# Keys and queries of later chunks transposed by VectorE instead of TensorE, and step sizes moved onto the keys

## The chip, the core and the metric

One core of a Trainium2 chip runs the whole program. The time is device microseconds of one execution, from the first to the last instruction and the little that lies around it. Three executions of the kernel before are given by their median. Engines are named as the profile names them: PE is TensorE's matmul, PEld its weight load, DVE is VectorE, ACT is ScalarE, POOL is GpSimd, SP is SyncE, which issues nearly all the transfers.

## What is computed

A delta-rule attention (4 batches, 8 heads, 768 positions, head size 48) gives 3072 rows of 384 numbers, which then go through two dense layers of width 2048, the first with mish, the second with hardswish:

```python
k_n = k / (norm(k) + 1e-06)
for t in range(S):
    y[:, :, t] = einsum('bhd,bhde->bhe', q[:, :, t], state)
    v_old = einsum('bhde,bhd->bhe', state, k_n[:, :, t])
    state = state + beta_t * einsum('bhd,bhe->bhde', k_n[:, :, t], v_t - v_old)
x = y reshaped to (3072, 384)
x = mish(x @ moe_w_in) @ moe_w_out            # 384 -> 2048 -> 384
x = hardswish(x @ moe2_w_in) @ moe2_w_out     # 384 -> 2048 -> 384
```

## The kernel before

The 768 positions are cut into 24 chunks of 32. A chunk holds its 4 batches as four groups of 32 partitions. For each chunk `t` the following is done.

- The keys are loaded by `load_heads` (L268, four transfers of 48 KB, one for each batch) into one of five tiles `kpad`, with positions on partitions; the queries go into one of two tiles `qpad`.
- TensorE turns both to have the head's 48 numbers on partitions: `T_pe` (L434) is four 128x128 transposes for the keys and four for the queries, and ScalarE copies each result from PSUM to `kqt` (`T_ew`, L440).
- `G_pe` (L454) multiplies keys with keys and keys with queries, into two PSUM banks. The first product, times the step sizes and a triangular mask `mb`, is the chunk's matrix `an`: VectorE forms it in `G_ew` (L472). The second becomes `mt`: ScalarE copies it (L483) and GpSimd masks it (L622).
- A unit triangular system with `an` is solved by 31 steps. For two chunks at a time, `an` goes to DRAM and back in another layout (`ad`, `ash`), VectorE multiplies (L785) and adds (L792) in each step, and the inverse goes to DRAM and back (`td`, `pt`). GpSimd multiplies `pt` with the step sizes (`scale`, L813).
- The recurrence `rec` then needs TensorE four times: K (`ksps`, L827), U (`ups`, L837), the output MU (`yps`, L847) and the state update S (`dsps`, L879), which VectorE adds to the state `sbd` in eight instructions (L890).

Chunks 0 to 7 are prepared ahead by other routines (`prep_k`, `matrices`, `whole`, `quads`). From chunk 8 on, the transposes of chunk `t + 4` stand directly behind U of chunk `t`, in the variable `tk` of `rec`. There are 16 such chunks.

Four chunks make a block of 512 columns for the dense layers. The first dense layer (phase 1) has six blocks of 16 units, each with nine matmuls into `hps` (L1205) and nine into `o` (L1226). The second (phase 2) begins when phase 1 ends. Before a unit of block 0 can run, its weights must be split into two rounded parts: ScalarE and VectorE do that in `lane` and `part` (L1139 to L1170). VectorE writes the last part of each of 28 pieces as `wil` or `wol` (L1170). The input of a block is split into `xh` (ScalarE) and `xl` (VectorE, L1187), into the same tiles for every block, after the last `hps` matmul of the block before.

All of this is written by one planner, `Flow`. Each routine is a generator that asks for an engine and a duration; the planner takes the request that could begin first, shifted by a penalty (`pen`), and writes its instructions there. So the order on every engine is fixed when the kernel is built, and each engine works through its own list in that order. `landed` and `DVE`/`ACT` numbers are the planner's assumptions of durations; changing them changes the order and nothing else. `warm` writes filler matmuls (L1544) until the first `hps`.

## Time and profile before

| | |
|---|---|
| median of 3 executions | 1038.71 us (1038.07 to 1043.14) |
| the profiled execution | 1040.45 us |
| its span, first to last instruction | 1038.7 us |
| PE busy | 1009.0 us, 97% |
| PEld busy | 842.5 us, 81% |
| DVE busy | 655.6 us, 63% |
| ACT busy | 452.0 us, 44% |
| POOL busy | 119.9 us, 12% |

The profiled execution's own time is 1.7 us over its span, and 1.7 us over the median. The span falls into stages: up to 89 us the first chunks and the first weights, without a dense layer on TensorE; from 89 to about 192 us block 0 of the first dense layer, while its weights are split; to 540 us blocks 1 to 4 with the rest of the attention; to 638 us the end of phase 1; to 1033.5 us phase 2. A share of busy time over the whole span mixes these, so the view of busy times by stretch, the list of waits, and the instructions in order of time around one step are what to read.

### The profile page before, as it was taken

The page shows a single profiled execution, that of the slowest core. Times are in us where ns is not written, and L with a number is a line of the kernel's source. Part 1 is how long each engine was busy: PE and PEld are TensorE (multiplying, and loading weights), DVE is VectorE, ACT ScalarE, POOL GpSimd, SP SyncE. Part 2 cuts the span into 40 slices and gives each one's busy share as a digit, 9 for nine tenths or more (in the row PEclk, how much of TensorE's full clock was granted, in tenths as well). Part 3 has the DMA queues.
Part 4 walks back from the last instruction along what each step waited for, and adds up shares of the span by engine and source line. Part 5 has one row for each costly group of instructions (what it writes and reads, how often), then busy time and mean ns, then how long its engine had stood idle before and what let it go on. Part 6 is the DMA issues. An engine that isn't in the chain of part 4 may idle for free.

```text
span 1038.7 us, 29553 instructions
## 1 busy us (share of the span) xinstructions
PE 1009.0 (97%) x12708; PEld 842.5 (81%) x12730; DVE 655.6 (63%) x1569; ACT 452.0 (44%) x916; POOL 119.9 (12%) x156
## 2 busy tenths in 40 slices
PE   8888999999999999999999999999999999999997
PEld 5466777787777878878778888998999989999997
DVE  7988999976869598596628888333343333433432
ACT  4454666534454354444236665333343333433432
POOL 3242333303121221210000000000000000000000
PEclk9999999999999999999999999999999999999999
DMA  4644553234242434414113643002020020100101
GB/s 87 158 97 103 152 129 99 78 57 77 42 95 41 76 54 87 74 20 89 22 44 121 203 137 107 1 1 62 1 61 1 1 61 1 37 25 1 31 1 32
DMA packets 149124, 66.58 MB, mean 64 GB/s; under 512 B 133088, under 2 KB 136160, under 8 KB 148992
## 3 DMA queue, kind: packets, MB, share of 16 engines
q1 hardware_dynamic: 147664, 64.19, 25.8%
q8 instruction: 100, 1.64, 0.7%
q10 hardware_dynamic: 1328, 0.49, 0.2%
q14 instruction: 32, 0.26, 0.1%
HBM read 51.02 MB, written 13.63 MB: 62 GB/s over the span
## 4 chain that ended last, share of the span: by engine, by line
PE 72%; DVE 16%; issue 2%; ACT 2%; DMA 1%; POOL 0%; SPq 0%; DVEq 0%; ACTq 0%
PE hps L1205 32%; PE p L1364 19%; PE o L1226 12%; DVE tmp L785 3%; DVE sbd L890 3%; DVE tp L792 3%; DVE cv L1147 1%; DVE cv L1150 1%; PE tps L434 1%; PE ksps L827 1%; PE ups L837 1%; PE yps L847 1%; PE dsps L879 1%; PE yps L827 1%; DVE glo L1245 1%
## 5 line engine op out<-in xcount | busy, mean ns | idle before, releaser
L1205 PE MATMUL hps<-xh,wih 128*128 128x512 f32 x576 | 229.5, 398 | 4.7 <-DVE an L472 1.8
L1205 PE MATMUL hps<-xl,wih 128*128 128x512 f32 x576 | 227.5, 395 | 2.3 <-DVE xl L1187 2.2
L1205 PE MATMUL hps<-xh,wil 128*128 128x512 f32 x576 | 227.3, 395 | 0.0
L1339 DVE SCALAR_TENSOR_TENSOR r<-r,hps 128x512 f32<-128x512 f32 x96 | 66.1, 688 | 181.6 <-ACT r L1337 181.4
L1337 ACT ACTIVATE r<-hps,half_c 128x512 f32<-128x512 f32 x96 | 66.1, 689 | 174.8 <-PE hps L1205 174.8
L1205 PEld LDWEIGHTS hps<-xh,wih 128*128 128x128 f32 x576 | 108.7, 189 | 27.5 <-DVE an L472 3.1
L1364 PE MATMUL p<-woh,glo 128*128 128x384 f32 x384 | 129.5, 337 | 0.0
L1364 PE MATMUL p<-woh,ghi 128*128 128x384 f32 x384 | 129.2, 337 | 0.0
L1364 PE MATMUL p<-wol,ghi 128*128 128x384 f32 x384 | 128.9, 336 | 0.0
L1205 PEld LDWEIGHTS hps<-xl,wih 128*128 128x128 f32 x576 | 108.7, 189 | 24.3 <-DVE xl L1187 5.0
L1205 PEld LDWEIGHTS hps<-xh,wil 128*128 128x128 f32 x576 | 108.6, 188 | 23.1
L1236 ACT ACTIVATE g<-hps 128x512 f32<-128x512 f32 x96 | 57.3, 597 | 132.0 <-PE hps L1205 130.2
L1226 PE MATMUL o<-ghi,wol 128*128 128x512 f32 x288 | 114.2, 396 | 0.1
L1226 PE MATMUL o<-ghi,woh 128*128 128x512 f32 x288 | 113.6, 394 | 0.0
L1345 DVE TENSOR_TENSOR glo<-r,ghi 128x512 fp32r<-128x512 f32 x96 | 66.5, 693 | 60.8 <-ACT ghi L1211 60.2
L1245 DVE TENSOR_TENSOR glo<-g,ghi 128x512 fp32r<-128x512 f32 x80 | 56.3, 704 | 75.4 <-ACT ghi L1211 75.0
L1211 ACT ACTIVATE ghi<-r 128x512 fp32r<-128x512 f32 x96 | 60.6, 632 | 70.4 <-DVE r L1339 70.4
L785 DVE TENSOR_TENSOR tmp<-tp,ash 128x126 f32<-128x126 f32 (+22 forms) x248 | 84.8, 342 | 8.8 <-DMA ash<-ad 2.5
L1226 PE MATMUL o<-glo,woh 128*128 128x512 f32 x288 | 84.3, 394 | 0.0
L1364 PEld LDWEIGHTS p<-woh,ghi 128*128 128x128 f32 x384 | 72.2, 188 | 4.0
L1364 PEld LDWEIGHTS p<-wol,ghi 128*128 128x128 f32 x384 | 72.1, 188 | 3.9
L792 DVE TENSOR_TENSOR tp<-tp,tmp 128x126 f32<-128x126 f32 (+22 forms) x248 | 69.3, 279 | 6.5
(148 smaller groups left out, 1384.0 us busy)
## 6 DMA issues: line engine op xcount, KB each, us to landing
raw<-in_moe_w_in_dram SPq DMA_DIRECT2D x24, 512.0 KB, 3.6
raw<-in_moe_w_out_dram SPq DMA_DIRECT2D x32, 384.0 KB, 3.2
vt<-in_v_dram SPq DMA_DIRECT2D x96, 48.0 KB, 2.4
x2d<-x2out SPq DMA_DIRECT2D x6, 768.0 KB, 3.8
x2in<-x2d SPq DMA_DIRECT2D x6, 768.0 KB, 5.5
kpad<-in_k_dram SPq DMA_DIRECT2D x92, 48.0 KB, 2.3
qpad<-in_q_dram SPq DMA_DIRECT2D x88, 48.0 KB, 2.5
ash<-ad SPq DMA_DIRECT2D x16, 256.0 KB, 4.0
```

What stands on the lines that cost most here:

```text
L785: nc.vector.tensor_tensor(out=tv, in0=x[:, 0:m, j:j + 1].to_broadcast([128, m, n]), in1=a[:, j + 1:C, j:j + 1].rearrange("p i o -> p o i") ...
L792: nc.vector.tensor_tensor(out=x[:, 0:m, j + 1:C], in0=x[:, 0:m, j + 1:C], in1=tv, op=ALU.add)
L890: nc.vector.tensor_tensor(out=o, in0=o, in1=S_part(b, r), op=ALU.add)
L1205: nc.tensor.matmul(out=ps[0], lhsT=w[:, kk, c], rhs=xhl[n][xi][:, kk, :], start=(kk == 0 and x == 0), stop=(kk == KD - 1 and x == 2))
L1211: nc.scalar.activation(out=hi, in_=g, func=ACTF.Copy)
L1226: nc.tensor.matmul(out=acc[i][dc], lhsT=w[:, e, 128 * dc:128 * (dc + 1)], rhs=a, start=(f == 0 and x == 0), stop=(f == KF - 1 and x == 2))
L1236: nc.scalar.activation(out=g, in_=ps, func=ACTF.Mish)
L1245: (nc.gpsimd if u < KF else nc.vector).tensor_tensor(out=lo, in0=g, in1=hi.bitcast(F32), op=ALU.subtract)
L1337: nc.scalar.activation(out=r, in_=ps, func=ACTF.Relu, scale=1.0 / 6.0, bias=half_c)
L1339: nc.vector.scalar_tensor_tensor(out=r, in0=r, scalar=1.0, in1=ps, op0=ALU.min, op1=ALU.mult)
L1345: nc.vector.tensor_tensor(out=lo, in0=r, in1=hi.bitcast(F32), op=ALU.subtract)
L1364: nc.tensor.matmul(out=acc[n][s], lhsT=a[:, c], rhs=w[:, e, :], start=(f == 0 and x == 0), stop=(f == KF - 1 and x == 2))
```

## The change

From chunk 8 on (`TD = 8`), TensorE transposes nothing. The two `qpad` tiles, free by then, become staging tiles: keys of a chunk are loaded a second time into the first, queries into the second, with 32 positions in a row of blocks, eight transfers for a chunk (four for each: rows of 32 numbers and of 16 numbers, for two halves of the heads). VectorE's transpose of 32x32 blocks writes them into `kqt` (`turns`). The tile `kqt` has its dimensions in another order. `kpad` is still loaded as before.

The step sizes move. The matrix `an` is now the raw product, copied by ScalarE, with the step sizes in its unused column 0. The 31 steps multiply by that column and read the matrix along rows, with one instruction of three operands for the multiplication (`scalar_tensor_tensor`) and a subtraction. The inverse is used without step sizes, so `scale` has no multiplication on GpSimd; instead ScalarE scales the keys in `kpad` (`scale_k`, eight instructions a chunk), and the mask that GpSimd multiplies into `mt` carries the step sizes too.

The fetch of the matrix is its own routine (`fetches`) with a second buffer, which the next pair of chunks uses while the steps of the pair before run. Penalties and assumed durations of the planner have other values.

```diff
-            for t in range(4, NS):
+            for t in range(4, TD):
                 yield f"Tq{t - NQP}"
                 yield LOAD
                 load_q(t)
+            for t in range(TD, NS):
+                yield f"S{t - 5}"
+                for i, src in ((0, k), (1, q)):
+                    yield f"Tq{TD - 2 + i}" if t == TD else f"kqt{t - 1}.{i}"
...
+                    for r in range(2):
+                        for d0, d1 in ((0, 32), (32, D)):
+                            nc.sync.dma_start(
+                                out=x[64 * r + d0:64 * r + d0 + C, :, 0:d1 - d0],
+                                in_=src[:, r::2, C * t:C * (t + 1), d0:d1].rearrange("b j s d -> s (b j) d"),
+                            )
...
+        def turns():
+            for t in range(TD, NS):
+                yield f"QS{t - NKQ}"
+                for i in range(2):
+                    yield f"raw{t}.{i}"
+                    yield "DVE.", 0.65
...
+                    nc.vector.transpose(out=kqt[t].rearrange("p b j i s -> p (b j) i s")[:, :, i, :], in_=raw_kq(i))
...
             for r in range(2):
-                yield "DVE.", 0.285
-                G_ew(t, r)
+                yield "ACT", 0.28
+                nc.scalar.activation(out=x[:, r::2, 1:C], in_=gps[t, r][:, :, 1:C], func=ACTF.Copy)
...
+        def scale_k():
+            for t in range(8, NS):
...
+                for h in range(H):
+                    yield "ACT", 0.28, 0
+                    x = kdata(t)[:, h, :]
+                    nc.scalar.activation(out=x, in_=x, func=ACTF.Copy, scale=bnat[:, t, h:h + 1])
+                flow.set(f"ks{t}")
...
+                own = "lo1.27" in flow.ev
+                tag = "r1" if own and g % 2 else "ash"
...
-                    nc.vector.tensor_tensor(
-                        out=tv,
-                        in0=x[:, 0:m, j:j + 1].to_broadcast([128, m, n]),
-                        in1=a[:, j + 1:C, j:j + 1].rearrange("p i o -> p o i").to_broadcast([128, m, n]),
-                        op=ALU.mult,
-                    )
...
+                    nc.vector.scalar_tensor_tensor(
+                        out=tv, in0=x[:, 0:m, j:j + 1].to_broadcast([128, m, n]), scalar=a[:, j, 0:1], op0=ALU.mult,
+                        in1=a[:, j:j + 1, j + 1:C].to_broadcast([128, m, n]), op1=ALU.mult)
...
-                yield "POOL", 0.62
-                nc.gpsimd.tensor_tensor(
-                    out=x[:, t], in0=x[:, t],
-                    in1=bnat[:, 2 * g + t, :].rearrange("p (h o) -> p h o", o=1).to_broadcast([128, H, C]),
-                    op=ALU.mult,
-                )
...
-                tk = t + 4 if 4 <= t < NS - 4 else None
+                tk = t + 4 if 4 <= t < TD - 4 else None
...
+                    if 8 <= t and not last:
+                        yield f"ks{t}"
```

Three places of the two orders follow. The first is TensorE's list at U of chunk 8 (`ups`), which stands behind the 23rd unit's `hps` before and behind the 21st's now. Before:

```order
L837 MATMUL ups<-r,pt 32x48 x32
L827 MATMUL yps<-sbd,kqt 32x96 x16
L434 MATMUL tps<-ident,kpad_104 128x128 x4
L434 MATMUL tps<-ident,qpad_107 128x128 x4
L1205 MATMUL hps<-xh,wih_2302 128x512
```

Now:

```order
L899 MATMUL ups<-r,pt 32x48 x32
L889 MATMUL yps<-sbd,kqt 32x96 x16
L1289 MATMUL o_4102<-ghi,woh_2037 128x512
L1289 MATMUL o_4102<-ghi,wol_2038 128x512
L1289 MATMUL o_4103<-ghi,woh_2037 128x512
```

The eight transposes are gone, and a dense layer's matmuls follow directly; U of chunk 8 stands two units earlier.

The second is VectorE's list at the 27th of the 28 weight pieces (the third `wol` of the last group), which unit 14 of block 0 waits for. `tmp` and `tp` are the solver's multiplication and addition, `cv` the weight split. Before:

```order
L1150 SCALAR_TENSOR_TENSOR cv<-raw,cv 128x384
L1170 TENSOR_TENSOR wol_3780<-cv,woh_3779 128x384
L785 TENSOR_TENSOR tmp<-tp,ash 128x128
L1141 TENSOR_SCALAR cv<-cv 128x384
L792 TENSOR_TENSOR tp<-tp,tmp 128x8x16
```

Now:

```order
L1213 SCALAR_TENSOR_TENSOR cv<-raw,cv 128x384
L856 SCALAR_TENSOR_TENSOR tmp<-tp,ash 128x110
L860 TENSOR_TENSOR tp<-tp,tmp 128x11x10
L1233 TENSOR_TENSOR wol_3823<-cv,woh_3822 128x384
L856 SCALAR_TENSOR_TENSOR tmp<-tp,ash 128x108
```

Ahead of this piece there stand now 44 solver instructions where there were 30, eight block transposes where there were none, none of the eight `an` products that stood there, and one `nn` reduction less (12 for 13).

The third is SP's list at the loads for one chunk in this stretch. Now, with `qpad_107` as staging tile for the keys and `qpad_108` for the queries:

```order
L269 DMA vt<-in_v_dram 32x8x48 x4
L1178 DMA raw<-in_moe_w_in_dram 128x1024
L1178 DMA raw<-in_moe_w_out_dram 128x768 x2
L269 DMA kpad_106<-in_k_dram 32x8x48 x4
L339 DMA qpad_107<-in_k_dram 32x16x32
L339 DMA qpad_107<-in_k_dram 32x16x16
L339 DMA qpad_107<-in_k_dram 32x16x32
L339 DMA qpad_107<-in_k_dram 32x16x16
L339 DMA qpad_108<-in_q_dram 32x16x32
```

Before, one group of four transfers of 32x8x48 into `qpad` stood for the queries; now there are eight transfers for a chunk, four of them with keys.

## Rows read from the trace of the kernel before

**Rows 1.** Busy times of the page: us (share of the span), instructions.

```profile
PE 1009.0 (97%) x12708; PEld 842.5 (81%) x12730; DVE 655.6 (63%) x1569; ACT 452.0 (44%) x916; POOL 119.9 (12%) x156
```

**Rows 2.** Busy us by stretch: length, PE, PEld, DVE, ACT, POOL, clock, DMA.

```profile
89.00:192.40 103.40, 99.29 (x2078) 78.75 (x2076) 96.67 (x225) 60.51 (x141) 36.79 (x32) 0.98 0.48 125
192.40:206.00 13.60, 12.00 (x42) 8.46 (x42) 12.38 (x35) 8.01 (x20) 3.60 (x2) 0.87 0.07 28
206.00:540.00 334.00, 330.09 (x5923) 265.61 (x5923) 238.95 (x729) 142.69 (x331) 52.12 (x71) 1.00 0.30 59
638.00:1033.50 395.50, 395.50 (x1991) 358.85 (x1989) 150.77 (x230) 138.68 (x220) 0.00 (x0) 1.00 0.08 22
```

**Rows 3.** Waits of PE, 90 to 600 us: total us, times, longest.

```profile
PE hps L1205 <- DVE xl L1187: 2.2, 4, 0.8
PE hps L1205 <- DVE an L472: 1.8, 3, 0.7
PE hps L1205 <- DVE late L738: 1.6, 1, 1.6
```

**Rows 4.** PE in order of time, U with transposes: start, us, instruction.

```profile
262.37 0.88 PE L837 MATMUL ups<-r,pt 32*32 32x48 f32 x64
263.19 0.66 PE L434 MATMUL tps<-ident,kpad 128*128 128x128 f32 x4
...
264.04 0.48 PE L1226 MATMUL o<-ghi,woh 128*128 128x512 f32 x1
```

**Rows 5.** PE in order of time, U of a chunk without transposes.

```profile
521.27 0.88 PE L837 MATMUL ups<-r,pt 32*32 32x48 f32 x64
522.08 0.50 PE L1226 MATMUL o<-ghi,wol 128*128 128x512 f32 x1
```

**Rows 6.** Tile tps, 90 to 460 us: count, duration min/median/max ns, first and last.

```profile
L440 ACT ACTIVATE kqt<-tps x32: 576/596/602, 106.7 to 455.6; 128x512 f32<-128x512 f32 x32
```

**Rows 7.** PE in order of time, end of block 0 and start of block 1.

```profile
192.98 0.50 PE L1226 MATMUL o<-ghi,wol 128*128 128x512 f32 x1
...
197.78 0.55 PE L1205 MATMUL hps<-xl,wih 128*128 128x512 f32 x1 [0.73 <-DVE xl L1187]
```

**Rows 8.** DVE in order of time, same place: the last two weight pieces.

```profile
192.36 0.56 DVE L1170 TENSOR_TENSOR wol<-cv,woh 128x384 fp32r<-128x384 f32 x1 [0.59 <-ACT woh L1167]
...
197.64 0.54 DVE L1170 TENSOR_TENSOR wol<-cv,woh 128x384 fp32r<-128x384 f32 x1
```

**Rows 9.** DVE groups: count, busy us, mean ns, idle before.

```profile
L716 DVE STREAM_TRANSPOSE z<-late 128x1024 f32<-128x1024 f32 x1 | 1.2, 1245 | 0.0
L1485 DVE STREAM_TRANSPOSE bst<-bst 128x640 f32<-128x640 f32 x1 | 0.8, 833 | 0.0
L718 DVE STREAM_TRANSPOSE late<-late 128x1024 f32<-128x1024 f32 x1 | 1.9, 1929 | 0.0
L472 DVE TENSOR_TENSOR an<-gps,mb 128x128 f32<-128x128 f32 x32 | 8.7, 283 | 2.5 <-ACT mt L483 2.5
L785 DVE TENSOR_TENSOR tmp<-tp,ash 128x126 f32<-128x126 f32 (+22 forms) x248 | 84.8, 342 | 8.8 <-DMA ash<-ad 2.5
L792 DVE TENSOR_TENSOR tp<-tp,tmp 128x126 f32<-128x126 f32 (+22 forms) x248 | 69.3, 279 | 6.5
```

**Rows 10.** ACT groups: count, busy us, mean ns, idle before.

```profile
L342 ACT ACTIVATE vt<-vt,nn 128x48 f32<-128x48 f32 x144 | 36.2, 322 | 0.6 <-DMA vt<-in_v_dram 0.5
L483 ACT ACTIVATE mt<-gps 128x128 f32<-128x128 f32 x40 | 9.1, 272 | 34.8 <-PE gps L454 34.8
```

**Rows 11.** Transfers by tile: count, KB each, median us to landing.

```profile
qpad<-in_q_dram SPq DMA_DIRECT2D x88, 48.0 KB, 2.5
pt<-td SPq DMA_DIRECT2D x8, 256.0 KB, 3.7
```

**Rows 12.** Waits of SP's own list: total us, times, longest.

```profile
SPq L268 <- PE tps L434: 54.7, 14, 10.5
```

More of the change, by code (lines that the diff above doesn't have):

```diff
@@ L21 @@
 NKQ = 4
+TD = 8
 RATE, TOKENS = 32.0, 110.0
@@ L316, in loads_k, with raw_kq @@
                     flow.ev[f"k{t}"] = flow.ev[f"kk{t}"]
+        def raw_kq(i):
+            return qpad[i].rearrange("p j r d -> p (j r d)").rearrange("p (n x) -> p n x", x=C)
         def loads_q():
-            for t in range(4, NS):
+            for t in range(4, TD):
                 yield f"Tq{t - NQP}"
@@ L322, in loads_q @@
                 load_q(t)
+            for t in range(TD, NS):
+                yield f"S{t - 5}"
+                for i, src in ((0, k), (1, q)):
+                    yield f"Tq{TD - 2 + i}" if t == TD else f"kqt{t - 1}.{i}"
+                    x = raw_kq(i)
+                    if t == TD:
+                        yield "POOL", 0.5
+                        for r in range(2):
+                            nc.gpsimd.memset(x[64 * r + 32:64 * r + 64, :, 16:32], 0.0)
+                    yield LOAD
+                    for r in range(2):
+                        for d0, d1 in ((0, 32), (32, D)):
[3 more added lines that the diff above has]
+                            )
+                    flow.ev[f"raw{t}.{i}"] = flow.landed(2.6)
+        def turns():
[4 more added lines that the diff above has]
+                    yield "DVE.", 0.65
+                    if i == 0:
+                        kqt[t] = ap_.tile([128, B, NP, 2, C], F32, tag=f"kqt{t % NKQ}", name="kqt")
+                    nc.vector.transpose(out=kqt[t].rearrange("p b j i s -> p (b j) i s")[:, :, i, :], in_=raw_kq(i))
+                    flow.set(f"kqt{t}.{i}")
+                flow.set(f"kq{t}")
         def loads_v():
@@ L438, in T_ew @@
             if i == 0:
-                kqt[t] = ap_.tile([128, NP, B, 2, C], F32, tag=f"kqt{t % NKQ}", name="kqt")
+                kqt[t] = ap_.tile([128, B, NP, 2, C], F32, tag=f"kqt{t % NKQ}", name="kqt")
             nc.scalar.activation(
                 out=kqt[t][:, :, :, i, :],
-                in_=tps.pop((t, i)).rearrange("p j (b s) -> p j b s", b=B),
+                in_=tps.pop((t, i)).rearrange("p j (b s) -> p b j s", b=B),
                 func=ACTF.Copy,
@@ L535, in matrices @@
                 yield "ACT", 0.6
-                x = ap_.tile([128, NP, B, 1, C], F32, tag=("tp", "an")[t % 2], name="kt")
-                nc.scalar.activation(out=x.rearrange("p j b o s -> p j (b o s)"), in_=tps.pop((t, 0)), func=ACTF.Copy)
+                x = ap_.tile([128, B, NP, 1, C], F32, tag=("tp", "an")[t % 2], name="kt")
+                nc.scalar.activation(out=x[:, :, :, 0, :], in_=tps.pop((t, 0)).rearrange("p j (b s) -> p b j s", b=B),
+                                     func=ACTF.Copy)
                 release(("T", t, 0))
@@ L827, in state_pe @@
                     nc.tensor.matmul(
-                        out=ps[C * b:C * (b + 1), j, :], lhsT=kqt[t][:, j, b, i, :], rhs=sbd[:, b, j, :],
+                        out=ps[C * b:C * (b + 1), j, :], lhsT=kqt[t][:, b, j, i, :], rhs=sbd[:, b, j, :],
                         start=(i == 0 or j == 0), stop=(i == 0), skip_group_check=True,
@@ L1523, in w1_pen @@
             if "moe1" not in flow.ev:
-                return 0.524
+                return 0.573
             idx = w1.next
             end = 7 * (idx // 7) + KD - 1
-            due = flow.ev["moe1"] + 24.438 * (idx // 7) - 2.164 * max(1, end - idx + 1)
-            return 0.025 if due - flow.free["DVE"] < 2.89 else 0.128
+            due = flow.ev["moe1"] + 23.217 * (idx // 7) - 2.5 * max(1, end - idx + 1)
+            return 0.025 if due - flow.free["DVE"] < 2.89 else 0.069
         def mish():
@@ L1551, in tile_delta_rule__moe_mish__moe_hardswish @@
         busy = lambda x, y: lambda: y if "moe1" in flow.ev else x
-        flow.add(norm4(0), pen=-0.3)
-        flow.add(norm4(1), pen=lambda: 0.0 if "D0" in flow.ev else 0.798)
+        flow.add(norm4(0), pen=-0.166)
+        flow.add(norm4(1), pen=lambda: 0.0 if "D0" in flow.ev else 0.821)
         for t in range(4):
-            flow.add(prep_k(t), pen=0.0)
-        flow.add(betas(), pen=0.0)
-        flow.add(matrices(), pen=lambda: 0.0 if "D0" not in flow.ev else 0.381)
+            flow.add(prep_k(t), pen=-0.106)
+        flow.add(betas(), pen=0.044)
+        flow.add(matrices(), pen=lambda: 0.0 if "D0" not in flow.ev else 0.399)
         flow.add(whole(), pen=-0.22)
-        flow.add(rec(), margin=busy(0.0, 1.05))
-        flow.add(scale_v(), pen=busy(0.54, 0.003))
+        flow.add(rec(), margin=busy(0.0, 1.039))
+        flow.add(scale_v(), pen=busy(0.581, 0.057))
         flow.add(loads_start())
```

89 lines of the change are left out of this document (57 added, 32 removed).

## The prediction

> **What bounds the kernel now.** I read the busy times first [rows 1], then the same by stretch [rows 2], then TensorE's waits [rows 3], then single steps in order of time. TensorE is the engine to watch: from 638 to 1033.5 us its busy time equals the stretch, and from 206 to 540 us it lacks 334.00 - 330.09 = 3.9 us [rows 2]. In those stretches time taken from TensorE's list is time taken from the end, as long as no other engine comes late. From 89 to 192.4 us it is different: TensorE lacks 4.1 us and VectorE only 103.40 - 96.67 = 6.7 us. Two engines are full there, and who waits for whom decides at the end of block 0: VectorE writes the 27th weight piece from 192.36 to 192.92, and TensorE's matmul that reads it starts at 192.98 [rows 7, 8]. The 28th piece and `xl` hold TensorE again until 197.78. So block 0 ends when VectorE has worked through its list.
>
> The Trainium skill (Perfetto Trace Analysis, Identifying the Most-Contended Engine) says that matmul busy time is a poor measure for TensorE, that its weight-load share is better, and that VectorE's occupancy is a fair one. By it TensorE is at 78.75 of 103.40 there, 76%, and VectorE at 93%, so VectorE is the fuller engine; the start at 192.98 agrees. In 206 to 540 the same measure gives TensorE 80% and VectorE 72%.
>
> **Transposes off TensorE.** With them, U begins at 262.37 and the dense matmul behind it at 264.04: 1.67 us [rows 4]. Without them, in a late chunk, the same takes 522.08 - 521.27 = 0.81 us [rows 5]. One chunk's eight transposes cost 0.86 us. The copies of their results are 32 in number, two for a chunk, between 106.7 and 455.6 us [rows 6]: 16 chunks, 16 x 0.86 = 13.8 us. They stand in TensorE's list between full stretches, so nothing hides them. Four of the 16 (chunks 8 to 11) lie before 192.4 us: 3.4 us. Twelve lie after: 10.3 us.
>
> **What VectorE gets and loses.** Two block transposes of 512 columns a chunk. No such row exists; 1024 columns take 1.25 us and 640 take 0.83, so 384 columns cost 0.41, and 512 come to 0.83 - 128 x 0.00107 = 0.70 us [rows 9]. A floor is half of 1.25, 0.62; the ceiling is half of the 1.93 us that a transpose with a strided input took, 0.96. Input and output here lie in runs of 32, near the first, so I take 0.70: 32 x 0.70 = 22.4 us. The `an` products go, 32 x 0.283 = 9.1 us. The solver's multiplication reads its matrix along a row instead of down a column: 248 instructions at 342 ns against 279 ns for the addition of the same sizes. If it comes down to the addition, 84.8 - 69.3 = 15.5 us are saved; if the third operand costs what the stride did, nothing. I take the first, since the rows differ in the stride and little else. Over the whole kernel VectorE changes by 22.4 - 9.1 - 15.5 = -2 us (between -5 and +22). From 206 us on it has 95 us to spare [rows 2], which hides either.
>
> In block 0 it is not hidden. Up to the 27th piece the list has 8 transposes more (5.6 us), 8 `an` products less (-2.3), one small reduction less (left out), and 44 solver instructions for 30. The 14 more cost 14 x 0.28 = 3.9, and the 15 multiplications among the first 30 save about 15 x 0.06 = 0.9: +3.0. In all +5.8 us of VectorE work. The bounds for what it does to the end of block 0: VectorE idles 6.7 us there, mostly waiting for partners; if all of that closed, the end would come 0.9 us earlier, if none, 5.8 us later. I take some three quarters of it as closing, since a later VectorE finds its inputs ready: +0.6 us. Then the 3.4 us that TensorE saves there are not seen: it waits for weights instead. The solver steps done early are steps that need not be done later, so chunk 8 stands two units earlier, but after 206 us VectorE's time is free anyway.
>
> **What the other engines get.** ScalarE loses 32 copies of 596 ns (19 us) and gains 32 copies of `an` at 272 ns (8.7), 16 short ones, and 128 key scalings at 322 ns, 41 us [rows 6, 10]: +34 us on 452, 2 us a chunk. It is busy 142.69 of 334 and 60.51 of 103.40 us [rows 2], so the cover is ample. S of a chunk now waits for its scaled keys. In ScalarE's list the scalings of each chunk from 8 on stand ahead of the copy of `u` of that chunk, by a whole step or more, so S should not feel them; behind the scalings queue the mish and the `u` copies, each late by 0.3 us at most per scaling. GpSimd loses the 16 products on `pt`; the mask product of `mt` only takes another mask. The `an` wait of the dense matmuls (1.8 us, three times [rows 3]: PSUM banks held until VectorE had read them) passes to ScalarE, which has more room; I count half of it, -0.9 us, with 0 and -1.8 as bounds.
>
> SP issues eight transfers a chunk where four stood for the queries. Their price is in time to landing: 2.5 us for 48 KB in 256 pieces, and 3.7 us for 2048 pieces of 128 bytes [rows 11]. The new ones have 512 pieces each and lie between. Covered by a chunk's period: 20 chunks from 89 to 540 us are 22.5 us each.
>
> The start to 89 us has the same instructions on VectorE and ScalarE up to the first `xl` and the first mish, 25 more fillers on TensorE in gaps, and some pieces in another order: 0, within 2 us either way. Phase 2 does not change.
>
> **The sum.** 1040.45 (profiled) - 13.8 + 3.4 + 0.6 - 0.9 = 1029.75. The profiled execution was 1.74 us above the median, so 1028.0 us, 10.7 us or 1.0% faster.
>
> **Rivals.** (a) Full gain. VectorE's +5.8 us is absorbed, block 0 ends 3.4 us earlier, and the `an` waits go: 1038.7 - 13.8 - 1.8 = 1023; with the 2.2 us of `xl` waits also gone, 1021. For it: VectorE's 6.7 us of idle time. Against it: the start 0.06 us behind the weight piece [rows 7, 8].
>
> (b) Block 0 late by all of 5.8 us, and new short waits of about 0.4 us at the 15 state updates behind ScalarE's longer list: 1038.7 - 13.8 + 3.4 + 5.8 + 6 = 1040, no change. For it: the scalings on the S path. Against: their early place and ScalarE's idle time.
>
> (c) Slower: the staging tiles. Keys of the next chunk may be loaded only when VectorE has turned the last, and SP works in order. The loop is 2 x 3.7 for the two loads, 1.4 for the transposes, and SP's wait before a load, 10.5 us at its longest so far [rows 12]: 19.3 us, under the period of 22.5. It decides from 22.5 on, since then chunks come late to their blocks. With a queue wait of 15 us the loop is 23.8 and 16 chunks lose 1.3 us each: 1028 + 21 = 1049. The Trainium skill (DMA: Bandwidth & Descriptors, Specifications) says that pieces under 512 bytes fall short of line rate. No run here shows a large-piece load of these tensors; the pieces were 192 bytes before and are 128 and 64 now.
>
> (d) The change doesn't do what it says: the three-operand multiplication is no faster. VectorE keeps 15.5 us, hidden after 206 us; in block 0, 22 multiplications at 0.06 are 1.3 us: 1029.3, inside the forecast's range.
>
> **How the numbers follow.** Forecast with (d), 1024.5 to 1033: 0.50. (a), 1019 to 1024.5: 0.31. (b), 1033.5 to 1043.5: 0.12. (c): 0.07. A measurement of this kernel can tell about 0.5% (5.2 us) from no change, so faster means below 1033.5: 0.81; same 0.12; slower 0.07. The range takes in the forecast, (a) down to 1020 and the lower part of (b): 1020 to 1036.
>
> **What would show it.** Right: no `tps` rows after 100 us; PE's busy time by stretch still nearly the stretch's length behind block 0, and blocks 1 to 5 shorter by about 10 us in all; `kqt<-qpad` transposes near 0.70 us; the three-operand multiplication near 280 ns; TensorE's waits in block 0 larger than 4.1 us and ended by the weight split; the first `xl` of block 1 at about the same time as before. Wrong: block 1 begins 3 us or more earlier (then (a)), waits of S on ScalarE or of transposes on transfers (then (b) or (c)), or a start later than 91 us.

## The result

The changed kernel takes 1052.22 us (median of four runs, 1048.17 to 1053.87) beside 1038.72 for the kernel before: 1.0115 times as long, 95% interval 1.0075 to 1.0155. It is slower, where 1028 was forecast and 1020 to 1036 was the range.

The traced execution is the fastest of the four (1048.17 us, span 1046.4). Its page answers [rows 1] with

```profile
PE 1003.3 (96%) x12600; PEld 833.4 (80%) x12627; DVE 654.2 (63%) x1569; ACT 468.7 (45%) x1060; POOL 107.7 (10%) x144
```

TensorE is busy 5.7 us less, though it runs more fillers, and ends 7.7 us later: it stands still 13.4 us longer. To see where, I split each trace at the first `hps` matmul of each block (a block has 144 of them): the start ends with the first one, blocks 1 to 4 hold the rest of the recurrence, phase 1 without it and phase 2 follow.

| kernel (traced execution) | start, us | block 0, us | blocks 1 to 4, us | all after, us |
|---|---|---|---|---|
| before | 89.0 | 105.9 | 369.7 | 474.1 |
| after | 95.7 | 111.9 | 365.0 | 473.8 |
| difference | +6.7 | +6.0 | -4.7 | -0.3 |

Busy us by stretch, block 0 and blocks 1 to 4 of the kernel after (columns as in [rows 2]):

```profile
95.70:207.60 111.90, 100.89 (x2058) 78.83 (x2053) 102.12 (x249) 70.24 (x190) 37.13 (x34) 0.94 0.53 123
207.60:572.60 365.00, 355.06 (x5970) 282.35 (x5969) 272.75 (x796) 177.31 (x480) 42.09 (x57) 1.00 0.39 76
```

The same cut of the kernel before:

```profile
89.00:194.90 105.90, 101.69 (x2087) 80.53 (x2085) 99.17 (x233) 62.19 (x144) 37.48 (x33) 0.98 0.47 122
194.90:564.60 369.70, 364.29 (x6065) 292.65 (x6064) 266.65 (x792) 163.90 (x373) 55.02 (x73) 1.00 0.31 64
```

And the `tps` transposes in it, length of the stretch and TensorE's busy time in them, which are all gone after (the time counts what the next matmul's record overlaps):

```profile
89.00:194.90 105.90, 4.37 (x32) 0.98 0.47 122
194.90:564.60 369.70, 13.11 (x96) 1.00 0.31 64
```

From the first transpose of a chunk to the matmul behind it, as in [rows 4], it is 0.85 us for each chunk: 10.2 us of the list in blocks 1 to 4 and 3.4 in block 0. So in blocks 1 to 4 TensorE's busy time falls by 9.2 us (the matmuls that stay take about 1 us more), its idle time rises from 5.4 to 9.9, and 4.7 us are left. In block 0 busy time falls by only 0.8 us, since the rest takes 2.6 us more at a granted clock of 0.94 for 0.98; idle time rises from 4.2 to 11.0, and 6.0 us are lost.

What TensorE waits for in block 0, 89 to 208 us (total us, times, longest):

```profile
PE hps L1268 <- ACT wih L1230: 6.4, 2, 3.2
PE gps L488 <- issue: 2.4, 1, 2.4
PE hps L1268 <- ACT an L644: 1.3, 1, 1.3
```

The `an` wait of [rows 3] has only changed its engine. Two waits for a weight piece are new, at 183.50 and 188.37 us, and one of 2.4 us for which the profile names no engine. The piece is written by ScalarE, which had waited for VectorE's part of the split (ScalarE in order of time):

```profile
182.82 0.63 ACT L1230 ACTIVATE wih<-cv 128x512 fp32r<-128x512 f32 x1 [3.68 <-DVE cv L1213]
```

Blocks 1 to 4, after (206 to 575 us), and the waits at the state `sbd` before (194.9 to 564.6 us):

```profile
PE hps L1268 <- DVE sbd L952: 2.7, 3, 1.8
PE ksps L889 <- DVE sbd L952: 2.1, 6, 0.4
PE hps L1268 <- DVE xl L1250: 1.9, 5, 1.0
```

```profile
PE ksps L827 <- DVE sbd L890: 0.8, 2, 0.4
PE hps L1205 <- DVE sbd L890: 0.3, 1, 0.3
```

The start, TensorE in order of time, before and after (start, us, instruction, idle before):

```profile
34.81 7.50 PE L1544 MATMUL warm<-late 128*128 128x512 bf16 x34 [0.16 <-issue]
43.73 0.88 PE L837 MATMUL ups<-vt,pt 32*32 32x48 f32 x64 [1.42 <-DVE pt L676]
```

```profile
37.64 14.41 PE L1607 MATMUL warm<-late 128*128 128x512 bf16 x65 [0.16 <-issue]
51.98 0.88 PE L899 MATMUL ups<-vt,pt 32*32 32x48 f32 x64
```

Before, the first state update waited for `pt`. After, `pt` is written at 44.96 to 45.56 us, and 65 fillers hold the update until 51.98:

```profile
44.96 0.60 DVE L728 TENSOR_TENSOR pt<-z,bnat 128x256 f32<-128x256 f32 x1
```

Groups of the kernel after that answer [rows 9] and [rows 10] (count, busy us, mean ns):

```profile
L354 DVE STREAM_TRANSPOSE kqt<-qpad 128x512 f32<-128x512 f32 x32 | 22.3, 702 | 0.3 <-issue 0.2
L856 DVE SCALAR_TENSOR_TENSOR tmp<-tp,ash 128x126 f32<-128x126 f32 (+22 forms) x248 | 80.9, 326 | 13.4 <-DMA ash<-ad 6.6 <-POOL tp L841 1.0
L676 ACT ACTIVATE kpad<-kpad,bnat 128x48 f32<-128x48 f32 x128 | 32.1, 323 | 30.8 <-DVE bnat L416 30.6
L644 ACT ACTIVATE an<-gps 128x124 f32<-128x124 f32 x32 | 8.7, 273 | 0.0
```

### The profile page after: what moved, and what is told of

It reads as the page before. It is cut to its first block, busy times and chain, and to the rows that moved or that the text cites. A ratio compares the mean times of both kernels' runs of the same rounds, so it can differ in the third digit from the quotient of the medians.

```text
span 1046.4 us, 29533 instructions
## 1 busy us (share of the span) xinstructions
PE 1003.3 (96%) x12600; PEld 833.4 (80%) x12627; DVE 654.2 (63%) x1569; ACT 468.7 (45%) x1060; POOL 107.7 (10%) x144
## 4 chain that ended last, share of the span: by engine, by line
PE 67%; DVE 21%; DMA 3%; SPq 3%; issue 3%; ACT 3%; POOL 0%; DVEq 0%; ACTq 0%; POOLq 0%
PE hps L1268 30%; PE p L1427 19%; PE o L1289 10%; DVE tmp L856 5%; DVE tp L860 4%; DVE sbd L952 4%; SPq L269 3%; PE warm L1607 2%; DVE glo L1308 1%; PE dsps L941 1%; PE gps L488 1%; PE ups L899 1%; DVE kqt L354 1%; DVE cv L1210 1%; DMA vt<-in_v_dram 1%
## 5 line engine op out<-in xcount | busy, mean ns | idle before, releaser
L1268 PEld LDWEIGHTS hps<-xh,wih 128*128 128x128 f32 x576 | 108.4, 188 | 36.7 <-ACT wih L1230 7.4
L1268 PEld LDWEIGHTS hps<-xh,wil 128*128 128x128 f32 x576 | 108.4, 188 | 23.7 <-DVE wil L1233 0.7
L1289 PE MATMUL o<-ghi,woh 128*128 128x512 f32 x288 | 114.6, 398 | 0.0
L856 DVE SCALAR_TENSOR_TENSOR tmp<-tp,ash 128x126 f32<-128x126 f32 (+22 forms) x248 | 80.9, 326 | 13.4 <-DMA ash<-ad 6.6
L1427 PEld LDWEIGHTS p<-woh,glo 128*128 128x128 f32 x384 | 72.0, 188 | 0.0
```

The costliest lines, as they stand in the source:

```text
L856: nc.vector.scalar_tensor_tensor(out=tv, in0=x[:, 0:m, j:j + 1].to_broadcast([128, m, n]), scalar=a[:, j, 0:1], op0=ALU.mult, in1=a[:, j:j ...
L1268: nc.tensor.matmul(out=ps[0], lhsT=w[:, kk, c], rhs=xhl[n][xi][:, kk, :], start=(kk == 0 and x == 0), stop=(kk == KD - 1 and x == 2))
L1289: nc.tensor.matmul(out=acc[i][dc], lhsT=w[:, e, 128 * dc:128 * (dc + 1)], rhs=a, start=(f == 0 and x == 0), stop=(f == KF - 1 and x == 2))
L1427: nc.tensor.matmul(out=acc[n][s], lhsT=a[:, c], rhs=w[:, e, :], start=(f == 0 and x == 0), stop=(f == KF - 1 and x == 2))
```

## The experiments

A stretch is read from one execution. Kernels with the same lists up to the end of block 0 had 111.8 to 116.2 us for it, so under 4.5 us is not read from that column alone; the medians decide. The kernel before was run again beside each group of runs, with medians of 1038.7 to 1041.2 us: a difference of medians from two groups carries that, and the ratios do not. The groups are e1 to e4, e5 to e8, e9 to e12, e13 to e16, e17 and e18. In e11_quarter_later, e13_no_scale and e15_td24_no_scale a part of the computation is left out. All, in us:

| run | start | block 0 | blocks 1 to 4 | median | ratio to before, 95% |
|---|---|---|---|---|---|
| e1_fillers | 90.7 | 116.2 | 365.7 | 1042.9 | 1.0011 to 1.0043 |
| e2_old_numbers | 89.6 | 121.5 | 364.7 | 1054.0 | 1.0091 to 1.0161 |
| e3_new_numbers | 94.6 | 102.0 | 374.5 | 1050.1 | 1.0058 to 1.0116 |
| e4_td12 | 101.5 | 105.6 | 370.2 | 1051.8 | 1.0071 to 1.0138 |
| e5_load22 | 89.7 | 115.3 | 360.4 | 1042.0 | 1.0001 to 1.0029 |
| e6_twice_b0 | 89.3 | 115.8 | 365.9 | 1047.0 | 1.0045 to 1.0089 |
| e7_twice_later | 92.2 | 111.8 | 381.8 | 1059.9 | 1.0156 to 1.0214 |
| e8_td12_load22 | 91.4 | 115.5 | 365.8 | 1048.6 | 1.0046 to 1.0096 |
| e9_td24 | 93.0 | 111.4 | 364.1 | 1044.4 | 1.0025 to 1.0069 |
| e10_solver_held | 91.9 | 114.6 | 367.6 | 1049.6 | 1.0046 to 1.0098 |
| e11_quarter_later | 88.9 | 112.1 | 363.4 | 1042.7 | 0.9990 to 1.0029 |
| e12_td24_old | 91.6 | 115.5 | 364.6 | 1047.4 | 1.0041 to 1.0080 |
| e13_no_scale | 90.2 | 115.2 | 360.7 | 1042.8 | 0.9996 to 1.0033 |
| e14_scale_pool | 92.4 | 115.4 | 364.4 | 1047.6 | 1.0052 to 1.0111 |
| e15_td24_no_scale | 92.0 | 116.9 | 362.7 | 1046.2 | 1.0034 to 1.0071 |
| e16_td24_scale_pool | 92.0 | 114.8 | 368.3 | 1050.9 | 1.0084 to 1.0123 |
| e17_old24_wait | 90.0 | 108.4 | 366.6 | 1041.1 | 0.9985 to 1.0028 |
| e18_old12_wait | 88.5 | 115.8 | 369.0 | 1050.0 | 1.0072 to 1.0122 |

### The start: fillers

```diff
-                nc.tensor.matmul(out=ps[:, 0:z.shape[1]], lhsT=z[:, 0:128], rhs=z, start=True, stop=True)
+                fill += 1
+                if not 73 <= fill <= 102:
+                    nc.tensor.matmul(out=ps[:, 0:z.shape[1]], lhsT=z[:, 0:128], rhs=z, start=True, stop=True)
```

> The changed kernel without 30 of the 65 filler matmuls that stand in TensorE's list just ahead of the first state update (the first ups); nothing else of any list differs. Theory (fillers): the list ahead ran about 6 us late and the fillers were counted out for a start that did not slip, so they hold the first update from 45.6 us, where its operand pt is there, to 52.0. Then the first update starts at 45.5 to 46.5, the first hps at 89 to 90.5 instead of 95.7, block 0 lasts as long as before this edit (110 to 113), and the time falls by 5.5 to 6.5 us. Rival (the solver's chain after it sets the end of the start-up, whatever the first update does): the first update is early, but the first hps comes at 94 or later, and the time falls by less than 2 us.

The first update starts at 45.62 and waits for `pt` again:

```profile
36.79 8.16 PE L1610 MATMUL warm<-late 128*128 128x512 bf16 x37
45.62 0.88 PE L899 MATMUL ups<-vt,pt 32*32 32x48 f32 x64 [0.67 <-DVE pt L728]
```

The first `hps` comes at 90.7, and the median falls by 9.4 us, more than the 6.4 us of fillers. The fillers are shown to be the cause of the late start. The traced execution is the slowest of the ten (1048.3), with the long block 0.

Which number makes them so many was asked from both sides: the new work under the old numbers, and the old work under the new ones.

These are three of the 19 lines, as e2 has them (e3 is the kernel before with the left sides):

```diff
-        return self.dma + 2.1
+        return self.dma + 3.0
...
-            return flow.landed(1.6)
+            return flow.landed(2.2)
...
-        flow.add(warm(), pen=busy(0.207, 0.973))
+        flow.add(warm(), pen=busy(0.389, 0.994))
```

> The changed kernel's work (block transposes on VectorE, copies on ScalarE, step sizes on the keys, second matrix buffer) under the planner numbers of the kernel before: the two landing estimates 3.0 and 2.2, and every penalty and margin that both kernels have. Theory (numbers): the later start comes from the numbers alone, so the first hps starts at 88 to 91 and the time is 1045 or less; block 0 keeps what the new work costs it, 108 to 113. Rival (work): the new work itself makes the start late, by queues that did not exist before, and the first hps starts at 94 or later, time 1048 or more.

> The kernel before with the planner numbers of the changed kernel (landing estimates 2.1 and 1.6, all penalties and margins that both have), none of its new work. Theory (numbers): the first hps starts at 94 to 97 and the time is 1043 to 1047, block 0 about as before (105 to 108). Rival (work): the first hps starts at 88 to 90.5, and the time stays within 2 us of the kernel before.

The start follows the numbers: 89.6 with the old ones, 94.6 with the new. The time does not: both mixtures are slower than the kernel before, by 1.26% and 0.87%. The new work under the old numbers loses it in block 0, 121.5 us with one wait of 10.8 us for `wih`; the old work under the new numbers has a block 0 of 102.0 us, but 4.1 of the 4.8 us that it loses in blocks 1 to 4 are one wait for `xl` behind the first `hps` of block 1. Up to that `xl` matmul it takes 106.6 us, and the kernel before 107.1: its block 0 is as long as before, and not shorter. One number alone:

```diff
-            return flow.landed(1.6)
+            return flow.landed(2.2)
```

> The changed kernel with one planner number put back: the estimate of one head load's spacing, 2.2 instead of 1.6 us. The planner then counts 48 fillers ahead of the first state update instead of 67 (the kernel before has 35). Theory (this one number makes the start late): 19 fillers of 0.22 us are gone, the first hps starts at 89 to 92 instead of 95.7, and the time is 3 to 7 us below the changed kernel's, if the other order that the number brings does no harm in block 0. Rival (the other numbers make it late too): the first hps starts at 94 or later.

The first `hps` is at 89.7 and the median 1042.0, 10.2 us below the changed kernel's, more than the theory's 3 to 7. With head loads believed to come every 1.6 us, the planner lists the first `gps` earlier in its own time and fills the wait for `pt` with 67 fillers by its own count where it had 35 (65 and 34 of them are in the traces); on the chip those `gps` end at 37.5 us instead of 34.7, and the fillers don't shrink.

### Block 0 and blocks 1 to 4: VectorE's list

```diff
-TD = 8
+TD = 12
```

> The changed kernel with the block transposes from the thirteenth chunk on instead of the ninth: the four chunks that are prepared in block 0 are transposed by TensorE again (4 more transpose groups of 0.86 us there, 3.4 us), and their raw loads and 8 VectorE transposes (8 x 0.7 = 5.6 us) leave block 0. Theory (VectorE in block 0): these transposes and the waits for their loads push the weight splits back, so without them the two waits for wih (6.4 us in sum) shrink to under 2, and block 0 lasts 104 to 109. Rival (copies and order): block 0 is long for the copies on ScalarE and the planner's order, and lasts 111 or more.

Block 0 lasts 105.6 as the theory had it, but the start is 101.5, so block 1 begins at 207.1 beside 207.6: nothing was gained, and the run decides nothing. The same with the start mended:

```diff
-TD = 8
+TD = 12
...
-            return flow.landed(1.6)
+            return flow.landed(2.2)
```

> The changed kernel with the head-load estimate of before (2.2 instead of 1.6) and the block transposes from the thirteenth chunk on, so that block 0 has neither raw loads nor VectorE transposes. Theory (start late by fillers, block 0 late by VectorE): the first hps starts at 89 to 92, block 0 lasts 104 to 108 and blocks 1 to 4 together 364 to 371, so the time is 1032 to 1041, no slower than before. Rival (the copies on ScalarE and the prefetched solver keep block 0 long): block 0 lasts 110 or more, the time is 1043 or more.

Block 0 stays at 115.5 without VectorE's transposes and without their loads. My theory of block 0 fell here.

Two runs put more of VectorE's work at an unchanged order:

```diff
-                    nc.vector.transpose(out=kqt[t].rearrange("p b j i s -> p (b j) i s")[:, :, i, :], in_=raw_kq(i))
+                    for _ in range(2 if t < 12 else 1):
+                        nc.vector.transpose(out=kqt[t].rearrange("p b j i s -> p (b j) i s")[:, :, i, :], in_=raw_kq(i))
```

> The kernel without the 30 fillers (e1_fillers), with each of the 8 block transposes of chunks 8 to 11, which lie in block 0, issued twice: 8 x 0.62 to 0.70 = 5.0 to 5.6 us more work for VectorE in block 0, no other row differs, and no transfer is added. Theory (VectorE's list bounds block 0): the end of block 0 moves by the added work, 4 to 8 us, and the time is 1047 to 1051 beside 1042.9 of e1_fillers; the waits of hps for wih grow. Rival (the weight splits are late for their raw loads, or for the order alone, and VectorE has slack): under 1.5 us, 1041 to 1044.5.

> The kernel without the 30 fillers (e1_fillers), with each of the 24 block transposes of chunks 12 to 23, in blocks 1 to 4, issued twice: 24 x 0.64 = 15.4 us more work for VectorE there (it is busy 275 of 365 us). Theory (there VectorE has room, and what of the gain is missing goes to short waits at single places): 0 to 3 us more than e1_fillers, 1042 to 1046. Rival (VectorE's list bounds blocks 1 to 4 as well): 6 to 15 us more, 1049 to 1058.

(e7_twice_later has `t >= 12` in place of `t < 12`.) In block 0, 8 x 0.70 = 5.6 us more cost 4.1 us: VectorE is full there, as the first part of the prediction had it. In blocks 1 to 4, 24 x 0.703 = 16.9 us more cost 17.0 us (16.4 by the ratios), although VectorE is busy for 272 of 365 us. My theory was wrong: a mean share of 75% is no room for a second dose. The waits are those at the state, which TensorE and VectorE hand to each other (208 to 590 us of e7_twice_later):

```profile
PE hps L1269 <- DVE sbd L953: 7.5, 3, 3.9
PE ksps L890 <- DVE sbd L953: 6.3, 14, 1.4
```

Whether the first dose costs anything is another question:

```diff
-                        kqt[t] = ap_.tile([128, B, NP, 2, C], F32, tag=f"kqt{t % NKQ}", name="kqt")
-                    nc.vector.transpose(out=kqt[t].rearrange("p b j i s -> p (b j) i s")[:, :, i, :], in_=raw_kq(i))
+                        kqt[t] = kqt[t - 4] if t >= 12 else ap_.tile([128, B, NP, 2, C], F32, tag=f"kqt{t % NKQ}", name="kqt")
+                    w = 16 if t < 12 else 4
+                    nc.vector.transpose(out=kqt[t].rearrange("p b j i s -> p (b j) i s")[:, 0:w, i, :], in_=raw_kq(i)[:, 0:w])
```

> The kernel without the 30 fillers (e1_fillers, 1042.9 us), in which each of the 24 block transposes of chunks 12 to 23 turns only a quarter of its columns (the other three quarters keep what chunks 8 to 11 left; this part of the computation is left out). The instructions, their order and the transfers stay. VectorE loses some 24 x 0.45 = 11 us in blocks 1 to 4. Theory (VectorE's list bounds these blocks, as the 17 us for 15.4 us of doubled transposes say): 8 to 13 us less, 1030 to 1035. Rival (VectorE had just no room for more, but the transposes as they are lie beside TensorE's work): 0 to 3 us less, 1040 to 1043.

1042.7 beside 1042.9 (1.8 us less by the ratios), where the theory had 8 to 13 less. The transposes of blocks 1 to 4 as they stand lie beside TensorE's work, and a second dose does not. Rival right, theory wrong.

And all transposes back on TensorE, the rest of the change kept:

```diff
-TD = 8
+TD = 24
...
-            return flow.landed(1.6)
+            return flow.landed(2.2)
```

> The changed kernel with the head-load estimate 2.2 (as e5_load22, 1042.0 us) and no VectorE transposes at all: all keys and queries are transposed by TensorE and copied by ScalarE, as before the change; the copies of the matrices on ScalarE, the scaled keys and the prefetched solver stay. VectorE loses 32 x 0.64 = 20.4 us, TensorE gets 16 x 0.86 = 13.8 to 16.4 us back. Theory (in blocks 0 to 4 VectorE's list binds as much as TensorE's, so the exchange is worth nothing): within 3 us of e5_load22, 1039 to 1045. Rival 1 (the transposes alone spoil the change): 1031 to 1036, block 0 under 108. Rival 2 (TensorE's work alone binds, as the prediction had it): 1052 to 1058.

1044.4 beside 1042.0 for e5_load22, in the theory's range: 13.6 us of transposes taken off TensorE's list (16 chunks at 0.85) are worth 2.4 us in the whole, 3.3 by the ratios. The order of the lists differs too. The trace shows the exchange. Without VectorE's transposes blocks 1 to 4 take 364.1 us, with nearly no idle time in them; with them, TensorE's busy time is 8.8 us less, its idle time 5.1 us more. By stretch, e9_td24:

```profile
204.40:568.50 364.10, 361.85 (x6065) 291.73 (x6064) 264.49 (x777) 192.43 (x515) 42.47 (x58) 1.00 0.33 71
```

And e5_load22:

```profile
205.00:565.40 360.40, 353.02 (x5969) 282.61 (x5968) 269.56 (x785) 178.02 (x480) 41.98 (x57) 1.00 0.40 77
```

### What makes block 0 long

First the solver, whose steps stand between the weight splits:

```diff
                 for j in range(C - 1):
+                    if g == 4 and j == 8:
+                        yield "lo1.26"
```

> The kernel without the 30 fillers (e1_fillers, 1042.9 us), with the triangular solver of chunks 8 and 9 held back in VectorE's list from its ninth step until the weight split 26 of 28 is listed; 10 of its 26 pairs of steps that stood ahead of block 1 move behind it, 10 x 0.6 = 6 us of VectorE's work. Theory (solver steps ahead of the weight splits make block 0 long): the waits of hps for wih fall from 6.5 us to under 2, block 0 gets 3 to 6 us shorter, and the time is 1037 to 1041. Rival (the work only moves, and block 1 gets longer by as much, for the state update of chunk 8 waits for the solver): 1041.5 to 1046.

Wrong: only 29 solver instructions stand ahead of block 1 where e1_fillers has 49, but the waits for `wih` are 7.7 us for 6.5, block 0 is as long, and the update of chunk 8 comes at 232.1 us for 223.3. The time is 1049.6, above the rival's range too.

Then ScalarE's new instructions, taken away or moved at an unchanged order:

```diff
                 for h in range(H):
                     yield "ACT", 0.28, 0
-                    x = kdata(t)[:, h, :]
-                    nc.scalar.activation(out=x, in_=x, func=ACTF.Copy, scale=bnat[:, t, h:h + 1])
+                nc.gpsimd.tensor_tensor(out=kdata(t), in0=kdata(t), op=ALU.mult,
+                                        in1=bnat[:, t, :].rearrange("p (h o) -> p h o", o=1).to_broadcast([128, H, D]))
```

e13 and e15 only lose the two lines with -, on e5_load22 and on e9_td24. e14 has the two lines with + as well, on e5_load22; e16 has them on e9_td24, with one slot of 0.83 us on GpSimd in the planner for ScalarE's eight, so that the whole order is another.

> The kernel with the head-load estimate 2.2 (e5_load22: 1042.0 us, block 0 115.3 us) without the scaling of the keys by their step sizes (8 ScalarE instructions for each of 16 chunks, 128 x 0.23 = 29 us of ScalarE's time, 7.3 us of it in block 0; this part of the computation is left out); no other row differs. Theory (these instructions stand in ScalarE's list ahead of steps of the weight splits for which VectorE waits): block 0 gets 4 to 8 us shorter, time 1034 to 1038. Rival (ScalarE, 62% busy in block 0, has room; block 0 is long for its order alone): 0 to 2 us, 1040 to 1043.

> The kernel with estimate 2.2 and all transposes on TensorE (e9_td24: 1044.4 us, block 0 111.4 us) without the scaling of the keys (left out, as in e13). Theory (ScalarE's list): block 0 lasts 104 to 108 us and the time is 1037 to 1041. Rival (order): block 0 stays at 110 to 112, 1042 to 1045.

> As e13, but the keys are scaled, by one GpSimd instruction for each chunk at the same place instead of ScalarE's eight (0.83 to 0.90 us by the like scaling of vt). Theory (ScalarE's list makes block 0 long): nearly the gain of e13, less what VectorE loses while GpSimd runs (16 x 0.9 us at most, 4 of them in block 0): 1035 to 1041, at or below the kernel before. Rival (VectorE stands still while GpSimd works, so it is no cheaper there): 1041 to 1046.

> As e9_td24 (estimate 2.2, all transposes on TensorE), with the keys scaled by one GpSimd instruction for each chunk that the planner knows of, so that the order is planned anew. What remains of the change: copies of the matrices on ScalarE, the three-operand multiply, the second matrix buffer. Theory (ScalarE's list made block 0 long, and blocks 1 to 4 gain some 5 us from the relieved VectorE): block 0 103 to 108, time 1031 to 1038. Rival (the order of the new planner numbers does it): block 0 110 or more, time 1042 or more.

Wrong in all four; e14_scale_pool and e15_td24_no_scale (1047.6 and 1046.2) lie above their rivals' ranges too. Without the scalings ScalarE has 7.2 us less to do in block 0 and 20.9 less in blocks 1 to 4, and nothing moves. Block 0 of e5_load22 by stretch, ScalarE's busy time the fourth:

```profile
89.70:205.00 115.30, 102.83 (x2056) 79.90 (x2054) 106.03 (x258) 70.17 (x190) 36.85 (x34) 0.93 0.51 120
```

And of e13_no_scale:

```profile
90.20:205.40 115.20, 102.89 (x2059) 79.95 (x2053) 105.72 (x257) 62.95 (x157) 36.14 (x32) 0.93 0.50 118
```

On GpSimd the same products cost 4.9 us beside e13_no_scale of the same group (e14_scale_pool; 5.6 beside e5_load22), more than on ScalarE, where they cost nothing.

What is left is the order. The kernel under all numbers of before (as e2_old_numbers) with all transposes on TensorE:

```diff
-TD = 8
+TD = 24
...
-            return flow.landed(1.6)
+            return flow.landed(2.2)
...
-        flow.add(warm(), pen=busy(0.207, 0.973))
+        flow.add(warm(), pen=busy(0.389, 0.994))
```

> The changed kernel under all planner numbers of the kernel before (as e2_old_numbers, 1054.0 us), with all transposes on TensorE. What differs from the kernel before is then the copies of the matrices on ScalarE, the scaled keys, the three-operand multiply and the second matrix buffer with its early fetch. Theory (VectorE's list bounds blocks 0 to 4; these parts relieve it by 6.7 us of copies and some 5 us of multiplies): first hps at 89 to 90, and 1030 to 1038, faster than the kernel before. Rival (the order that goes with them puts the solver ahead of the weight splits in block 0, as in e2_old_numbers): block 0 lasts 112 or more, the time is 1043 to 1052.

1047.4 us, block 0 115.5: the rival. It differs from the kernel before in few things, one of them a condition that the change drops; put back:

```diff
                     if tg:
                         yield f"kq{tg}"
+                        yield f"mb{tg}"
```

> e12_td24_old (planner numbers of before, all transposes on TensorE; 1047.4 us, block 0 115.5 us) with the one condition put back that the change dropped: the state products of a chunk are listed only when the mask mb of the chunk three further on is there. The work is the same; 19 of the 61 solver steps that were listed ahead of block 1 stand behind its beginning. Theory (the order that follows from the dropped condition makes block 0 long): block 0 lasts 105 to 110 us, and the time falls by 4 to 9 us, to 1038 to 1043. Rival (the order is another but the lists are as badly matched to the chip): block 0 112 or more, time within 3 us of 1047.

1041.1 us, 6.3 less, block 0 108.4. The trace has 39 solver instructions ahead of block 1 instead of 62 (34 before the change), and the waits at the weights (2.9 us) are gone. e12_td24_old, then e17_old24_wait, 89 to 208 us:

```profile
PE ksps L889 <- DVE sbd L952: 2.7, 4, 1.6
PE o L1289 <- DVE wol L1233: 1.8, 1, 1.8
PE hps L1268 <- DVE late L790: 1.6, 1, 1.6
...
PE o L1289 <- ACT woh L1230: 1.1, 1, 1.1
```

```profile
PE ups L899 <- DVE r L1004: 2.5, 1, 2.5
PE hps L1269 <- DVE xl L1251: 1.7, 3, 1.2
PE hps L1269 <- DVE late L790: 1.6, 1, 1.6
```

So in this pair, whose work is the same, the order that follows from the dropped condition costs the 6.3 us (5.7 by the ratios). The number of solver steps ahead of block 1 alone is not it: e10_solver_held has 29 and a block 0 of 114.6. All this is shown for the old numbers with TensorE's transposes. With VectorE's from the thirteenth chunk on, and the scalings listed at once, it is not enough:

```diff
-TD = 24
+TD = 12
...
                 for h in range(H):
-                    yield "ACT", 0.28, 0
                     x = kdata(t)[:, h, :]
```

> The changed kernel with the planner numbers of before, the dropped condition on mb put back, the scaling of the keys listed at once and not slot by slot, and VectorE's transposes from the thirteenth chunk on only. Theory (order): first hps at 89 to 91, block 0 104 to 108, blocks 1 to 4 357 to 364 us: 1026 to 1036, faster than both kernels. Rival (any order that was not tuned for the new work runs into stalls that the planner doesn't see): block 0 112 or more, or blocks 1 to 4 above 367, time 1041 to 1050.

1050.0, block 0 115.8: the rival again. No version here beats the kernel before. Of those that leave nothing out, e17_old24_wait (0.9985 to 1.0028) is level with it.

## Why the prediction was wrong

The traced execution took 18.4 us more than the forecast gives for it (span 1046.4 for 1038.7 - 10.7 = 1028.0): 6.7 in the start, 5.4 in block 0, 5.6 in blocks 1 to 4, 0.9 for `an` waits that were to go, less 0.3 after them.

**The start** was taken as "0, within 2 us either way", and 25 more fillers as standing "in gaps". This step failed: 6.7 us in the trace, and 9.4 us of the median go with 30 fillers (e1_fillers). A filler stands in an in-order list, and it lies in a gap only while the list runs as planned. The row to look at was the number of fillers ahead of the first `ups`, against the time at which `pt` comes.

**Block 0** was given +0.6 us out of -0.9 to +5.8; it was +6.0. The mechanism was the one named (TensorE waits for the weight split, 6.4 us), but at two `wih` pieces some 20 us ahead of the end and not at the 27th piece; the size was the bound of the first half of rival (b). That a later VectorE would find its inputs ready and close three quarters of its idle time is the step that failed: it idled 9.8 us after and 6.7 before, in the two block 0 rows above. The +5.8 us of work was off as well. Its terms as written add up to 6.3 (5.8 only with the small reduction taken off, which the text leaves out), and VectorE's busy time in block 0 rose by 2.95 us. So more work for VectorE is not the cause, or not alone: without the transposes, without ScalarE's scalings, with the solver held back, block 0 stayed at 111 to 117 us. Shown is that VectorE has little room there (4.1 us for 5.6), and, for one pair, that the order of the lists is worth 6.3 us. Which part of the order does it in the changed kernel under its own numbers stays open.

**The transposes** cost TensorE what the sum had: 10.2 us of its list in blocks 1 to 4 for 10.3. 4.7 us of it arrived, and 9.3 in e5_load22. The step that failed is that time taken from TensorE's list there is time taken from the end. The prediction had it "as long as no other engine comes late", and VectorE came late at the state: of the 4.5 us that TensorE idles more, 3.7 are waits for `sbd` (4.8 us for 1.1). Why it comes late stays open, for with a quarter of the transposes the time is nearly the same. "From 206 us on it has 95 us to spare" was right for what the change put there (e11_quarter_later) and wrong as a reserve (e7_twice_later: 17.0 us for 16.9).

**The multiplication** was to fall from 342 to 279 ns; it fell to 326, 3.9 us saved instead of 15.5. The stride is gone and a third operand has come, and no run here parts the two. Rival (d) was right on this, and that it mattered little behind block 0 fits e11_quarter_later, where less work for VectorE saved next to nothing.

**The `an` waits** were to halve, -0.9 us; they went from 1.8 us on VectorE to 1.3 on ScalarE in block 0.

**Right**: block transposes at 0.70 us (702 ns); copies and scalings on ScalarE at 273 and 323 ns, with cover (e13_no_scale: nothing); phase 2 unchanged; no chain over the staging tiles, rival (c): VectorE's transposes waited 0.3 us in all. Rival (b)'s 6 us of short waits at the state came as 3.7, on VectorE's `sbd` and not on ScalarE's keys. Rival (b), 1040 by the median of before, with the late start added comes to 1046.7, or 1048.4 on the scale of the traced execution, which took 1048.2; that is luck, since neither its cause in block 0 nor its waits were those found.

The traced execution explains 7.7 us of the 13.5 between the medians. The other three runs of the changed kernel were 3.7 to 5.7 us longer, and no trace shows where.

## What to carry to other kernels

Where a program is listed by a planner, count what stands ahead of the first use in each in-order list, fillers too: a shorter estimate of a load buys nothing on the chip and fixes a longer wait into the list. A mean busy share of 75% on the partner engine of a recurrence says neither that it is full nor that it has room; halve and double the work on it at an unchanged order before trading work between engines. And when a change edits the conditions under which steps are listed, compare the lists first and the instructions second: the same work took 6.3 us more for one dropped condition.

## What the runs showed of the hardware

Products on GpSimd hold up some of VectorE's instructions. In the kernel after, a `cv` step takes 0.35 us while GpSimd is still (it does nothing from 183.5 to 190 us) and 1.45 us when it begins beside a GpSimd product; the two end 0.2 us apart, at 170.50 and 170.29:

```profile
187.78 0.35 DVE L1204 TENSOR_SCALAR cv<-cv 128x384 f32<-128x384 f32 x1
...
169.05 1.45 DVE L1204 TENSOR_SCALAR cv<-cv 128x384 f32<-128x384 f32 x1
```

```profile
168.89 1.40 POOL L1308 TENSOR_TENSOR glo<-g,ghi 128x512 fp32r<-128x512 f32 x1 [3.73 <-ACT ghi L1274]
```

The block transposes are not held up: none of the 32 in the kernel after took over 0.72 us. In e14_scale_pool one that begins with a GpSimd product takes 0.71 us; the solver step behind it takes 0.87 us beside the next product, and one of more columns 0.30 just before:

```profile
241.48 0.30 DVE L856 SCALAR_TENSOR_TENSOR tmp<-tp,ash 128x78 f32<-128x78 f32 x1
...
242.00 0.71 DVE L354 STREAM_TRANSPOSE kqt<-qpad 128x512 f32<-128x512 f32 x1
242.63 0.87 DVE L856 SCALAR_TENSOR_TENSOR tmp<-tp,ash 128x70 f32<-128x70 f32 x1
```

```profile
242.00 0.61 POOL L456 TENSOR_TENSOR mb<-masku,bnat 128x256 f32<-128x256 f32 x1 [1.72 <-DVE bnat L416]
242.57 0.83 POOL L675 TENSOR_TENSOR kpad<-kpad,bnat 128x384 f32<-128x384 f32 x1
```

That 16 such products of 0.90 us made e14_scale_pool 4.9 us longer than e13_no_scale fits this. The Trainium skill (Perfetto Trace Analysis, Optimizing Scalar/DVE Operations) says that work moved between these two engines may not help, since they share a read port; the trace agrees for the `cv` and the solver step, and shows no such cost for the transpose.

A wait of TensorE costs more than its length. Behind the 3.15 us wait in block 0 the same matmuls take 0.63 us for 0.39:

```profile
179.96 0.39 PE L1268 MATMUL hps<-xh,wil 128*128 128x512 f32 x1
183.50 0.80 PE L1268 MATMUL hps<-xh,wih 128*128 128x512 f32 x1 [3.15 <-ACT wih L1230]
184.09 0.63 PE L1268 MATMUL hps<-xl,wih 128*128 128x512 f32 x1
```

The granted clock from 183.5 to 190 us is 0.50, the lower of the two levels (1.2 GHz; 1 is the upper, 2.4). From 175 to 200 us, with two such waits, its mean is 0.80, and 0.96 in the kernel before. The stretches after, then the one before (columns as in [rows 2]):

```profile
183.50:190.00 6.50, 3.28 (x7) 1.88 (x8) 6.50 (x21) 1.68 (x3) 0.00 (x0) 0.50 0.38 112
175.00:200.00 25.00, 18.63 (x69) 14.11 (x68) 23.38 (x61) 13.83 (x36) 7.14 (x6) 0.80 0.37 99
```

```profile
175.00:200.00 25.00, 23.22 (x183) 17.35 (x183) 23.20 (x59) 12.51 (x30) 9.40 (x6) 0.96 0.23 54
```
